# w_in's row blocks dealt to the partitions in another order, and x permuted to match

## The chip, the core and the metric

The kernel runs on one core of one Trainium2 chip. The core has a matrix engine (TensorE, PE), a vector engine (VectorE, DVE), a scalar engine (ScalarE, ACT), a general engine (GpSimd, POOL), a queue engine that issues transfers (SyncE, SP), an on-chip memory of 128 partitions (SBUF), an accumulator memory that the matrix engine writes to (PSUM), and 16 DMA engines that move data between the chip's main memory (HBM) and SBUF. The metric is the device time of one execution in microseconds (us), lower being better. The time before is the median of three runs, 216.86 us (216.77 to 216.94).

## What is computed

One decoding step for two sequences: an attention over the last 4096 positions of a key and value cache, and a small gated network whose output, passed through silu, scales the attention's. Cut to what matters:

```python
def reference(A_x, A_k_cache, A_v_cache, A_wq, A_wo, B_x, B_w_in, B_w_sp, B_b_sp, B_w_out):
    def _A_ref(x, k_cache, v_cache, wq, wo):
        W = min(4096, max(256, Sk // 4))
        q = (lambda x, *d: x.transpose(*d))((x @ wq).reshape(B, Sq, Hq, Dh), 0, 2, 1, 3)
        k = jnp.repeat(k_cache[:, :, Sk - W:, :], rep, axis=1)
        v = jnp.repeat(v_cache[:, :, Sk - W:, :], rep, axis=1)
        scores = jnp.einsum("bhqd,bhkd->bhqk", q, k) * (Dh ** -0.5)
        p = _softmax(scores, axis=-1)
        o = jnp.einsum("bhqk,bhkd->bhqd", p, v)
        return (lambda x, *d: x.transpose(*d))(o, 0, 2, 1, 3).reshape(B, Sq, Hq * Dh) @ wo
    def _B_ref(x, w_in, w_sp, b_sp, w_out):
        z = _gelu(jnp.einsum("bsd,df->bsf", x, w_in))
        z1 = z[..., :Fh]
        z2 = _layernorm(z[..., Fh:], axis=-1)
        g = jnp.einsum("ts,bsf->btf", w_sp, z2) + b_sp[None, :, None]
        return jnp.einsum("bsf,fd->bsd", z1 * g, w_out)
    xn = _layernorm(A_x, axis=-1)
    s = _A_ref(xn, A_k_cache, A_v_cache, A_wq, A_wo)
    g = _silu(_B_ref(xn, B_w_in, B_w_sp, B_b_sp, B_w_out))
    return A_x + s * g
```

The batch is 2, D is 512, there are 32 query heads over 8 key and value heads of 128, and w_in is 512 x 1792. All numbers are float32.

## The kernel before

The kernel is a stream of large loads with the computing hung on their landings. All large loads are issued by SP in one order and move through the same 16 DMA engines: w_in (`win`), w_out (`wout`), wq in three pieces, then the windows of the caches, two key heads (K) or two value heads (V) at a time, in eight units each, and at the end wo. `win`, the pieces of wq, the K and V units and wo share a ring of four buffers (`slot`), so that SP issues a load when the buffer's previous tenant has been used up. The first K buffer is free from the beginning; its issue nevertheless stands behind a wait for win's landing.

The layout of a load is a mapping from rows in HBM to partitions. For w_in (lines 120 to 122) partition p gets the rows 4p to 4p + 3 (KT is 4), one run of 4 x 1792 floats, 28,672 bytes. Both sides of that load have 128 entries in their outermost dim. The K and V loads (lines 146 to 152) interleave two heads: their source has 64 entries outermost, then 2, then a run of 8192 floats, for 128 partitions.

x is normalized on two partitions as `xn` (line 194). A matmul contracts over partitions, so x is brought to them in the same order as the weights' rows: line 197 transposes, for each k of 0 to 3, the columns 4p + k of `xn` to partition p, and line 198 copies the result from PSUM into `xnT`, a tile of 128 x 4 x 32 whose other columns are zero. `xnT` is used twice: with `win` in lines 238 to 244 (`z`, four column blocks times four k, each k to its own quarter of the PSUM partitions), and with wq in `queries` (line 268), where wq's rows have the same order.

DVE, ACT, PE and SP work strictly in the order of the program (`InOrder`, line 55); POOL's memsets are placed by a scheduler. Between line 198 and the loop over `z` DVE builds a set of small constant masks. From the units on, the order of work is written out by hand in `ORDER`. PSUM tiles made with `bank` take turns in two buffers, and `kts` tiles likewise in SBUF.

The line of nearly every instruction in the profile is L65, the helper of `InOrder`; instructions are told apart by their tiles.

Of the kernel before, what the change touches and what calls it, by code (L numbers as in the profile page):

```python
# [9 lines left out]
F32 = mybir.dt.float32  # L10
# [4 lines left out]
P = 128  # L15
# [55 lines left out]
def kernel(  # L71
# [13 lines left out]
    nc = tc.nc  # L85
    pe, dve, act, sp = (InOrder(tc, e) for e in (nc.tensor, nc.vector, nc.scalar, nc.sync))
    B, _, D = x.shape
# [5 lines left out]
    F = w_in.shape[1]  # L93
    FH = F // 2
    KT = D // P
    FC = F // G
# [10 lines left out]
    cst = ctx.enter_context(tc.tile_pool(name="cst", bufs=1))  # L107
    sb = ctx.enter_context(tc.tile_pool(name="sb", bufs=2))
    ps = ctx.enter_context(tc.tile_pool(name="ps", bufs=1, space=bass.MemoryType.PSUM))

    def slot(name, *shape):
        return ring.tile([P, *shape], F32, tag="slot", name=name)

    def bank(name, *shape):
        return ps.tile([P, *shape], F32, tag="kt", name=name, bufs=2)


    xs = sb.tile([B, D], F32, tag="ss", name="xs", bufs=1)
    act.dma_start(xs, x[:, 0, :])
    win_v = w_in.rearrange("(p k) f -> p k f", p=P)  # L120
    win = slot("win", KT, F)
    sp.dma_start(win, win_v)
    wout = kts.tile([P, FT, D], F32, tag="kts", name="wout")
    sp.dma_start(wout, w_out.rearrange("(p j) d -> p j d", p=P))
    wq_v = wq.rearrange("(p k) f -> p k f", p=P)
# [29 lines left out]
    ident = cst.tile([P, P], F32, tag="ident", name="ident")  # L155
    make_identity(nc, ident)
    selw = cst.tile([P, 60], F32, tag="selw", name="selw")
    nc.gpsimd.memset(selw, 0.0)
    xnT = cst.tile([P, KT, 32], F32, tag="xnT", name="xnT")
    nc.gpsimd.memset(xnT, 0.0)  # L160
    ones = cst.tile([P, P], F32, tag="ones", name="ones")
    nc.gpsimd.memset(ones, 1.0)
# [29 lines left out]
    rsqrt(rs, va, "x")  # L192
    xn = sb.tile([B, D], F32, tag="o", name="xn", bufs=1)
    dve.tensor_scalar(xn, xs, mv[:, 0:1], rs, op0=ALU.subtract, op1=ALU.mult)
    pt = bank("xnT_ps", KT, B)
    for k in range(KT):
        pe.transpose(pt[:, k, :], xn.rearrange("b (p k) -> b k p", k=KT)[:, k, :], ident[:B, :B])
    dve.tensor_copy(xnT[:, :, :B], pt)

    same = cst.tile([P, G, 32], F32, tag="same", name="same")  # L200
    dve.tensor_copy(same, free_ap(rowm, 0, [[0, G], [1, 32]]))
# [24 lines left out]
    for nj in (8, 16):  # L226
        nx = 32 // nj
        to = cst.tile([P, nj * P // 32 // 4, 4, nx], F32, tag=f"perm{nj}", name=f"perm{nj}")
# [9 lines left out]
    for n in range(G):  # L238
        pz = bank(f"z{n}", 512)[:, :FC]
        for k in range(KT):  # L240
            pe.matmul(
                pz[32 * k : 32 * k + 32, :], xnT[:, k, :], win[:, k, n * FC : (n + 1) * FC],
                start=True, stop=True,
            )
        if n % 2:
            dve.tensor_copy(z[:, n * FC : (n + 1) * FC], pz)
        else:
            act.activation(z[:, n * FC : (n + 1) * FC], pz, AF.Copy)
# [4 lines left out]
    pt = bank("zT_ps", 2, FT, B)  # L253
# [349 lines left out]
    for u in range(NU):  # L603
        p = Unit()
        p.u, p.m, p.kt, p.sh, p.ss, p.s, p.p, p.pT = u, None, {}, {}, {}, {}, {}, {}
        units.append(p)
    for line in ORDER.strip().split("\n"):
        for name in line.split():
            name, at = name.split(":")
# [35 lines left out]
```

## Time and profile before

| | |
|---|---|
| median of three runs | 216.86 us (216.77 to 216.94) |
| the profiled execution | 217.29 us, of which its span 215.5 us |
| PE busy | 143.2 us, 66% of the span |
| DVE busy | 126.7 us, 59% |
| ACT busy | 51.6 us, 24% |
| POOL busy | 4.5 us, 2% |
| read from HBM | 89.40 MB, 415 GB/s over the span |
| mean granted clock of PE | 0.825 |

The span runs from the first to the last instruction of the program; the execution's own time is a little longer, as it holds what lies around that. Busy shares are averages over the whole span. "Idle before, and what ended it" in square brackets behind an instruction names what the instruction last waited for. The 16 DMA engines are shown together: their share is the mean over all of them.

### The profile page before, as it was taken

The page shows a single profiled execution, that of the slowest core. Times are in us where ns is not written, and L with a number is a line of the kernel's source. Part 1 is how long each engine was busy: PE and PEld are TensorE (multiplying, and loading weights), DVE is VectorE, ACT ScalarE, POOL GpSimd, SP SyncE. Part 2 cuts the span into 40 slices and gives each one's busy share as a digit, 9 for nine tenths or more (in the row PEclk, how much of TensorE's full clock was granted, in tenths as well). Part 3 has the DMA queues.
Part 4 walks back from the last instruction along what each step waited for, and adds up shares of the span by engine and source line. Part 5 has one row for each costly group of instructions (what it writes and reads, how often), then busy time and mean ns, then how long its engine had stood idle before and what let it go on. Part 6 is the DMA issues. An engine that isn't in the chain of part 4 may idle for free.

```text
span 215.5 us, 2332 instructions
## 1 busy us (share of the span) xinstructions
PE 143.2 (66%) x900; PEld 48.1 (22%) x900; DVE 126.7 (59%) x218; ACT 51.6 (24%) x129; POOL 4.5 (2%) x17
## 2 busy tenths in 40 slices
PE   0179796833854966964991795389259917987793
PEld 0117622111120221222220231123112201232231
DVE  2611213169899799649928972993698099636011
ACT  5011103300116036033330602142051206142201
POOL 8000000000000000000000000000000000000000
PEclk9999569665998896796697599669755997996999
DMA  7999999999999999999999999999999999999990
GB/s 246 432 443 444 398 429 465 414 458 414 456 408 447 420 426 444 426 443 426 450 420 450 408 441 420 426 450 426 447 415 456 401 456 414 447 426 417 420 374 22
DMA packets 3930, 89.54 MB, mean 416 GB/s; under 512 B 446, under 2 KB 462, under 8 KB 848
## 3 DMA queue, kind: packets, MB, share of 16 engines
q1 hardware_dynamic: 3900, 89.40, 96.8%
q8 instruction: 7, 0.11, 0.2%
q14 instruction: 3, 0.02, 0.0%
q10 hardware_dynamic: 20, 0.01, 0.0%
HBM read 89.40 MB, written 0.00 MB: 415 GB/s over the span
## 4 chain that ended last, share of the span: by engine, by line
DMA 63%; PE 23%; DVE 8%; ACT 3%; issue 1%; ACTq 0%
DMA v<-in_A_v_cache_dram 42%; DMA k<-in_A_k_cache_dram 16%; PE acc L65 10%; DMA win<-in_B_w_in_dram 5%; PE sh L65 5%; DVE kts L65 4%; PE part L65 4%; PE s L65 3%; DVE pT L65 1%; ACT p L65 1%; ACT o L65 1%; DVE gate L65 1%; PE mo L65 1%; ACT ss L65 1%; DVE qb L65 1%
## 5 line engine op out<-in xcount | busy, mean ns | idle before, releaser
L65 DVE STREAM_TRANSPOSE kts<-k 128x1024 f32<-128x1024 f32 x64 | 75.6, 1218 | 29.5 <-DMA k<-in_A_k_cache_dram 29.5
L65 PE MATMUL sh<-kts,qb 128*32 128x512 f32 x256 | 41.6, 775 | 13.2 <-DVE kts L65 9.3
L65 PE MATMUL acc<-v,pT 128*32 128x512 f32 x256 | 37.4, 707 | 8.8 <-DVE pT L65 4.4
L65 ACT ACTIVATE p<-s,nb 128x512 f32<-128x512 f32 x32 | 22.5, 733 | 36.2 <-DVE nb L65 36.2
L65 ACT ACTIVATE ss<-sh 128x512 f32<-128x512 f32 x16 | 9.6, 599 | 59.1 <-PE sh L65 59.1
L65 DVE STREAM_TRANSPOSE pT<-p 128x1024 f32<-128x1024 f32 x16 | 19.6, 1225 | 2.3 <-ACT p L65 2.1
L65 PE MATMUL s<-ss,sums 128*128 128x512 f32 x32 | 18.8, 671 | 2.3 <-ACT ss L65 2.3
L65 PE MATMUL mo<-mg,joint 128*128 128x16 f32 x16 | 4.0, 327 | 23.4 <-DVE mg L65 23.4
L65 PEld LDWEIGHTS acc<-v,pT 128*32 128x32 f32 x256 | 10.5, 145 | 35.1 <-issue 27.0
L65 PEld LDWEIGHTS sh<-kts,qb 128*32 128x32 f32 x256 | 8.8, 126 | 34.2 <-issue 28.8
L65 DVE TENSOR_REDUCE m<-s 128x1 f32<-128x512 f32 x16 | 10.7, 671 | 4.2 <-PE s L65 4.2
L65 PE MATMUL q_ps<-wq,xnT 128*32 128x512 f32 x64 | 10.5, 784 | 3.5 <-DMA wq<-in_A_wq_dram 3.5
L65 ACT ACTIVATE o<-acc,wd 128x128 f32<-128x128 f32 x32 | 9.1, 368 | 15.0 <-PE acc L65 15.0
L65 PEld LDWEIGHTS mo<-mg,joint 128*128 128x128 f32 x16 | 3.2, 250 | 27.2 <-DVE mg L65 24.4
L65 PE MATMUL z<-win,xnT 128*32 128x448 f32 x32 | 5.6, 869 | 4.7 <-DMA win<-in_B_w_in_dram 4.7
L65 PE MATMUL part<-wo,oT 128*32 128x512 f32 x56 | 7.7, 596 | 1.4 <-ACT o L65 1.4
L65 PEld LDWEIGHTS s<-ss,sums 128*128 128x128 f32 x32 | 5.0, 197 | 10.3 <-issue 7.7
L65 PE MATMUL zT_ps<-rowm,z 128*128 128x2 f32 x28 | 6.6, 370 | 0.0
L65 PEld LDWEIGHTS zT_ps<-rowm,z 128*128 128x128 f32 x28 | 6.5, 325 | 0.0
L65 ACT ACTIVATION_READ_ACCUMULATOR p<-s,nb 128x1 f32 x32 | 6.5, 203 | 0.0
L65 ACT ACT_TABLE_LOAD x4 | 5.1, 1283 | 2.6 <-POOL hT L164 2.6
L65 DVE COPY z<-z 128x448 f32<-128x448 f32 x2 | 1.3, 626 | 7.5 <-PE z L65 7.5
(111 smaller groups left out, 68.4 us busy)
## 6 DMA issues: line engine op xcount, KB each, us to landing
k<-in_A_k_cache_dram SPq DMA_DIRECT2D x8, 4096.0 KB, 27.4
v<-in_A_v_cache_dram SPq DMA_DIRECT2D x8, 4096.0 KB, 29.8
wq<-in_A_wq_dram SPq DMA_DIRECT2D x1, 4096.0 KB, 24.5
wq<-in_A_wq_dram SPq DMA_DIRECT2D x2, 2048.0 KB
wo<-in_A_wo_dram SPq DMA_DIRECT2D x1, 4096.0 KB, 30.4
win<-in_B_w_in_dram SPq DMA_DIRECT2D x1, 3584.0 KB, 11.5
wo<-in_A_wo_dram SPq DMA_DIRECT2D x1, 2048.0 KB
wout<-in_B_w_out_dram SPq DMA_DIRECT2D x1, 1792.0 KB, 15.3
```

Of the source, the lines that this page charges most:

```text
L65: return self.tc.keep_in_program_order(call(*args, **kwargs))
```

## The change

The source of w_in's load gets three dims instead of two: 16 entries one block (four rows) apart, within each 8 entries 16 blocks apart, and within each the run of a block. The destination is the same tile in the same order of partitions. So partition 8e + i holds block e + 16i, where before it held block 8e + i.

The contraction over w_in needs x in the same order. A copy on DVE permutes `xn`'s columns into a new tile `xp` on two partitions, four transposes bring them to the 128 partitions, and a copy puts them into a new tile `xnS`, which is set to zero by POOL beforehand and which the matmuls with `win` read. `xnT` is still made, after it, for wq. The number of matmuls is the same but for these four transposes.

```diff
-    win_v = w_in.rearrange("(p k) f -> p k f", p=P)
+
     win = slot("win", KT, F)
-    sp.dma_start(win, win_v)
+    spaced = [[KT * F, 16], [16 * KT * F, P // 16], [1, KT * F]]
+    sp.dma_start(win.rearrange("p k f -> p (k f)"), bass.AP(tensor=w_in.tensor, offset=w_in.offset, ap=spaced))
...
     xnT = cst.tile([P, KT, 32], F32, tag="xnT", name="xnT")
+    xnS = cst.tile([P, KT, 32], F32, tag="xnS", name="xnS")
+    nc.gpsimd.memset(xnS, 0.0)
     nc.gpsimd.memset(xnT, 0.0)
...
-    pt = bank("xnT_ps", KT, B)
-    for k in range(KT):
-        pe.transpose(pt[:, k, :], xn.rearrange("b (p k) -> b k p", k=KT)[:, k, :], ident[:B, :B])
-    dve.tensor_copy(xnT[:, :, :B], pt)
+    xs = sb.tile([B, KT, 16, P // 16], F32, tag="xp", name="xp", bufs=1)
+    dve.tensor_copy(xs.rearrange("b k e i -> b e i k"), xn.rearrange("b (i e k) -> b e i k", e=16, k=KT))
+    for to, of in ((xnS, xs.rearrange("b k e i -> b k (e i)")), (xnT, xn.rearrange("b (p k) -> b k p", k=KT))):
+        pt = bank("xnT_ps", KT, B)
+        for k in range(KT):
+            pe.transpose(pt[:, k, :], of[:, k, :], ident[:B, :B])
+        dve.tensor_copy(to[:, :, :B], pt)
...
-                pz[32 * k : 32 * k + 32, :], xnT[:, k, :], win[:, k, n * FC : (n + 1) * FC],
+                pz[32 * k : 32 * k + 32, :], xnS[:, k, :], win[:, k, n * FC : (n + 1) * FC],
```

## The prediction, made before the change was run

> **What bounds the kernel now.** I read the page first: the span, the transfer rows over the slices, the queues and the chain that ended last.
>
> ```profile
> span 215.5 us, 2332 instructions
> DMA  7999999999999999999999999999999999999990
> q1 hardware_dynamic: 3900, 89.40, 96.8%
> DMA 63%; PE 23%; DVE 8%; ACT 3%; issue 1%; ACTq 0%
> ```
>
> The sixteen DMA engines are busy in every slice but the first and the last, and the chain that ended last is transfers for 63% of the span. No compute engine stands near that. So the second view is the table of stretches, which gives the bytes moved in each (last column, GB/s) and the mean busy share of the DMA engines (next to last).
>
> ```profile
> 1.00:1.50 0.50, 0.00 (x0) 0.00 (x0) 0.00 (x0) 0.00 (x0) 0.47 (x4) 1.00 0.00 0
> 1.50:2.00 0.50, 0.00 (x0) 0.00 (x0) 0.35 (x2) 0.00 (x0) 0.50 (x4) 1.00 3.29 811
> 2.00:2.50 0.50, 0.00 (x0) 0.00 (x0) 0.50 (x3) 0.00 (x0) 0.50 (x1) 1.00 0.25 57
> 2.50:3.00 0.50, 0.00 (x0) 0.00 (x0) 0.47 (x2) 0.43 (x1) 0.50 (x1) 1.00 0.17 57
> 3.00:3.25 0.25, 0.00 (x0) 0.00 (x0) 0.18 (x2) 0.25 (x1) 0.25 (x1) 1.00 0.00 0
> 3.25:3.50 0.25, 0.00 (x0) 0.00 (x0) 0.00 (x0) 0.25 (x1) 0.25 (x1) 1.00 0.54 229
> 3.50:3.75 0.25, 0.00 (x0) 0.00 (x0) 0.00 (x0) 0.25 (x1) 0.25 (x2) 1.00 1.62 688
> 3.75:4.00 0.25, 0.00 (x0) 0.00 (x0) 0.00 (x0) 0.24 (x2) 0.25 (x3) 1.00 1.61 688
> 4.00:4.25 0.25, 0.00 (x0) 0.00 (x0) 0.00 (x0) 0.23 (x2) 0.25 (x2) 1.00 0.00 0
> 4.25:4.50 0.25, 0.00 (x0) 0.00 (x0) 0.00 (x0) 0.25 (x1) 0.25 (x2) 1.00 0.80 344
> ...
> 40.00:80.00 40.00, 23.73 (x142) 6.68 (x134) 32.58 (x42) 7.58 (x20) 0.00 (x0) 0.82 1.00 432
> 80.00:120.00 40.00, 27.23 (x166) 8.11 (x169) 28.87 (x41) 10.49 (x29) 0.00 (x0) 0.78 1.00 432
> 120.00:160.00 40.00, 26.15 (x168) 8.27 (x164) 28.73 (x40) 12.93 (x35) 0.00 (x0) 0.80 1.00 432
> ```
>
> From 40 to 160 us the rate is 432 GB/s at a share of 1.00, or 27.0 GB/s an engine: nothing is to be had there but fewer bytes, and the change moves the same bytes. The first microseconds are different. w_in goes over as 128 rows of 28,672 bytes, and a short stretch credits a packet whole to the moment it begins, so GB/s times the stretch, divided by 28,672, counts the packets that begin in it. 1.50 to 2.00 gives 405 KB, 14 packets; the next two stretches give one each: sixteen, the first packet of each engine. Then 2, 6, 6 and, after a hole, 3 begin: the second packets, and in the last group a third one of the engine that was ahead. With the middle of each stretch the first packets begin at 1.84 us on average ((14 x 1.75 + 2.25 + 2.75) / 16) and the second ones at 3.78 ((2 x 3.375 + 6 x 3.625 + 6 x 3.875 + 2 x 4.375) / 16). A first packet thus took 1.94 us, where 28,672 bytes at 27.0 GB/s are 1.06. **The start costs 0.88 us an engine on average, and the engines leave it about 1.0 us apart** (second packets begin at 3.4 to 4.4). As every engine has the same bytes to move at the same rate, the one that leaves last stays last, and a load has landed only when its last engine is done.
>
> The third view is that chain in order of time, for what the end hangs on.
>
> ```profile
> 0.73 11.48 DMA win<-in_B_w_in_dram
> ...
> 150.21 32.33 DMA v<-in_A_v_cache_dram
> ...
> 206.95 3.64 PE part L65 x28
> ```
>
> win lands at 12.2, which is 4.4 plus seven packets of 1.06 and 0.4 more. The last transfer on the chain lands at 182.54; the remaining 30 us are computing. The DVE work that this computing also needs had begun with another landing:
>
> ```profile
> 172.91 1.25 DVE L65 STREAM_TRANSPOSE kts<-k 128x1024 f32<-128x1024 f32 x1 [6.66 <-DMA k<-in_A_k_cache_dram]
> ```
>
> So whatever the first load gains or loses on its slowest engine passes through the full queues to those landings and to the end, one for one.
>
> **The change part by part.** It deals w_in's blocks (four rows each) so that partition 8e + i gets block e + 16i, and permutes x alike.
>
> *What is added beside the load.* These rows show the nearest work, and what covers it.
>
> ```profile
> 1.09 0.20 POOL L160 MEMSET xnT<- 128x128 f32 x1
> 2.56 1.28 ACT L65 ACT_TABLE_LOAD   x1 [2.56 <-POOL hT L164]
> 3.07 0.14 DVE L65 TENSOR_SCALAR va<-mv 2x1 f32<-2x1 f32 x1
> 6.33 0.53 DVE L65 TENSOR_SCALAR xn<-xs,mv,rs 2x512 f32<-2x512 f32 x1
> 7.01 0.61 PE L65 MATMUL xnT_ps<-ident,xn 2*128 2x2 f32 x4 [7.01 <-DVE xn L65]
> 7.65 0.17 DVE L65 COPY xnT<-xnT_ps 128x8 f32<-128x8 f32 x1 [0.79 <-PE xnT_ps L65]
> 9.57 0.28 DVE L65 TENSOR_REDUCE at<-ident 128x2 f32<-128x128 f32 x1
> 12.35 2.47 PE L65 MATMUL z<-win,xnT 128*32 128x448 f32 x12 [4.73 <-DMA win<-in_B_w_in_dram]
> 15.62 0.62 DVE L65 COPY z<-z 128x448 f32<-128x448 f32 x1 [5.77 <-PE z L65]
> 47.34 1.19 DVE L65 TENSOR_TENSOR qb<-qa,grpm 128x1024 f32<-128x1024 f32 x1
> ```
>
> One more memset on POOL is 0.20 us. It can delay the identity and with it DVE's first work, but va is done at 3.21 and ACT's logarithm cannot begin before its table is in at 3.84, so 0.6 us of delay is free. The permuting copy of 2 x 512 on DVE is not in the trace: 0.53 by the row of xn, 1.19 by the dearest strided row, which has twice the elements; I take 0.6, nearer the first, as it has xn's shape. Four transposes more are 0.61 on PE, one copy more is 0.17 on DVE. xnS is then ready at 7.82 + 0.6 = 8.4 (9.0 at most), xnT at about 9.2, and DVE's constants end near 11.3 instead of 9.85. PE's first matmul on win waits for the load until 12.35, and DVE has nothing to do until 15.62. Cost: nothing, with 3.3 us of cover; without that cover it would be 1.4 us on z alone. Even z being late would not reach the end, for the next rows show how deep the queue is.
>
> ```profile
> SPq L65 <- DMA win<-in_B_w_in_dram: 8.8, 1, 8.8
> win<-in_B_w_in_dram SPq DMA_DIRECT2D x1, 3584.0 KB, 11.5
> wout<-in_B_w_out_dram SPq DMA_DIRECT2D x1, 1792.0 KB, 15.3
> wq<-in_A_wq_dram SPq DMA_DIRECT2D x1, 4096.0 KB, 24.5
> wq<-in_A_wq_dram SPq DMA_DIRECT2D x2, 2048.0 KB
> k<-in_A_k_cache_dram SPq DMA_DIRECT2D x8, 4096.0 KB, 27.4
> ```
>
> The only issue that hangs on win's landing is the first of k. Ahead of it stand 13,568 KB, at 432 GB/s 32 us of work, while the issue comes at 12.2: it may come 20 us later without a gap.
>
> *The issue itself.* The source becomes a pattern of three dims, as k's is.
>
> ```profile
> 0.73 0.39 SPq L65 DMA_DIRECT2D win<-in_B_w_in_dram  x1
> L65 SPq DMA_DIRECT2D k<-in_A_k_cache_dram x8: 534/535/636, 12.2 to 145.5; - x8
> ```
>
> win's issue takes 0.39 us, k's 0.535. If the longer pattern is the reason, all packets begin 0.15 us later; the bounds are 0 and 0.25 (the longest of k's). It stands ahead of the very first packet, where nothing hides it. I take +0.15.
>
> *The start.* If each engine takes eight partitions in a row, the engines began 229,376 bytes apart, and now 28,672 apart. What that does to the 0.88 us no row shows. Bounds: the slowest engine's second packet begins at 4.4, and with no stall at all it would begin at 1.84 + 1.06 = 2.9, a gain of 1.5; if the stall grew by as much again as its mean, a loss of 0.9. Between, the nearest row is the engine that got through quickest, at 3.4, which is 1.0 better than the slowest: engines under the same start can do it. I take 0.7 of that, since an even start takes away crowding and not the latency that the quickest one has too.
>
> [...]
>
> Sum: -0.7 + 0.15 = -0.55 us. The profiled execution took 217.29 us, 1.8 more than its span of 215.5 and 0.43 more than the median of 216.86; taken off that median, the forecast is **216.3 us**, and 216.7 for an execution like the profiled one.
>
> **The rivals.** *The start stays as it was:* the delay is that of a cold start, whatever the addresses. For it: even the quickest engine lost 0.5 us (3.4 less 2.9). Against it: the 1.0 us between engines, which a common latency doesn't make. Time: 216.86 to 217.0 with the issue.
>
> *Neighbours crowd more:* sixteen engines now begin within 459 KB, and if they meet in the same part of memory the stall grows, by up to its mean of 0.88. It decides once the growth exceeds the 0.3 us that a measurement can see beside the issue. For it: the trace shows that a common start is uneven. Against it: after one packet all engines run at full rate whatever they read. Time: 217.3 to 217.8.
>
> *The split collides at the destination:* this is the rival that is far on the other side. The outermost dim of the source now has 16 entries where the destination has 128, so an engine may be given eight neighbouring partitions, and if two engines then write into the same part of SBUF at a time, each runs at half rate for the whole of win. Price: 3584 KB take 8.5 us at 432 GB/s, and 17.0 at 216, so +8.5: 225.4; with collisions for a part of the eight rows, less. It decides from the first packet, and win would land near 20 instead of 12.2. [...] Against it: k's source, with 64 entries outermost, already differs from its 128 partitions and runs at 432.
>
> [...]
>
> **How the numbers follow.** An uneven start cured: 0.37. Start as it was: 0.17. Neighbours crowd more: 0.16. Collision at the destination: 0.30. The forecast is the first, with its own range of 215.6 to 216.4 (a gain of 1.25 down to 0.45). About 0.2%, 0.43 us, is what a measurement of this kernel can tell from no change. Faster than that has 0.37, within it 0.19 (the second case and the small end of the third), slower 0.44. As cases of both signs hold most of the chance, the range for 8 times in 10 must reach into the fourth: 215.8 to 225.5.
>
> **What would show it.** In the table of stretches after: second packets that begin by 3.7 at the latest and closer together, win landing at about 11.5, every later landing earlier by as much, PE still waiting for win and not for xnS. A landing of win at 12.2 to 12.4 is the second case; 12.6 to 13.3 with full rate from the second packet the third; about 216 GB/s until 20 us the fourth. The forecast is wrong too if win lands early and the chain that ended last no longer passes through a load of v near 182, so that the gain is lost in the computing behind it.

## The result, and the profile after

The changed kernel takes 225.54 us (median of 4 runs, 225.32 to 225.55) where the kernel before takes 216.81 us (4 runs, 216.60 to 216.94): slower by 4.0%, ratio 1.0399 with a 95% interval of 1.0387 to 1.0412. That is 8.73 us more. The profiled execution took 225.53 us.

The page of the changed kernel, its span, transfer rows and queues:

```profile
span 223.7 us, 2344 instructions
...
DMA  7979989999899999999999999999999899999991
GB/s 165 246 164 287 492 381 422 460 428 464 381 463 445 404 460 404 439 463 385 457 428 422 463 393 448 457 398 457 416 431 458 387 463 439 410 460 404 428 395 42
...
q1 hardware_dynamic: 3900, 89.40, 96.9%
```

The GB/s row of the kernel before:

```profile
GB/s 246 432 443 444 398 429 465 414 458 414 456 408 447 420 426 444 426 443 426 450 420 450 408 441 420 426 450 426 447 415 456 401 456 414 447 426 417 420 374 22
```

The packets and bytes are the same, and the share in which the DMA engines are busy is the same as well (96.9% and 96.8%). Only the GB/s row tells the two kernels apart: its first four slices, some 22 us, move 165, 246, 164 and 287 GB/s where they moved 246, 432, 443 and 444. Here a busy share of 96.9% does not tell how fast the packets get through.

The stretches of the changed kernel, with busy share and GB/s in the last two columns:

```profile
2.00:2.50 0.50, 0.00 (x0) 0.00 (x0) 0.50 (x3) 0.00 (x0) 0.50 (x2) 1.00 3.27 860
2.50:3.00 0.50, 0.00 (x0) 0.00 (x0) 0.47 (x2) 0.29 (x1) 0.50 (x1) 1.00 0.22 57
...
3.75:4.00 0.25, 0.00 (x0) 0.00 (x0) 0.00 (x0) 0.24 (x2) 0.25 (x3) 1.00 3.90 803
4.00:4.25 0.25, 0.00 (x0) 0.00 (x0) 0.00 (x0) 0.23 (x2) 0.25 (x3) 1.00 3.34 688
4.25:4.50 0.25, 0.00 (x0) 0.00 (x0) 0.00 (x0) 0.25 (x1) 0.25 (x1) 1.00 1.68 344
...
5.00:19.00 14.00, 1.02 (x8) 0.96 (x8) 4.11 (x24) 0.70 (x2) 0.16 (x1) 1.00 0.95 197
...
80.00:120.00 40.00, 32.02 (x208) 9.71 (x212) 32.83 (x45) 11.45 (x31) 0.00 (x0) 0.87 1.00 432
```

The first of the long stretches, in the kernel before:

```profile
5.00:19.00 14.00, 7.26 (x42) 3.12 (x42) 4.59 (x25) 1.65 (x4) 0.01 (x1) 1.00 0.98 423
```

From 5 to 19 us, while only win is moving, the rate is 197 GB/s at a busy share of 0.95, so some 207 GB/s at full share, and a packet of 28,672 bytes takes 2.2 us on one of sixteen engines; from 80 us on it is 432 as before. In the same way as in the prediction, the packets that begin can be counted: sixteen by 3.00 us, sixteen more between 3.75 and 4.50, and then a hole before the next (0 GB/s from 4.50 to 5.00). What followed the load, in the order of time:

```profile
0.73 0.70 SPq L65 DMA_DIRECT2D win<-in_B_w_in_dram  x1
...
8.45 0.17 DVE L65 COPY xnS<-xnT_ps 128x8 f32<-128x8 f32 x1 [0.74 <-PE xnT_ps L65]
...
20.74 0.58 SPq L65 DMA_DIRECT2D k<-in_A_k_cache_dram  x1
...
20.86 1.72 PE L65 MATMUL z<-win,xnS 128*32 128x448 f32 x8 [11.98 <-DMA win<-in_B_w_in_dram]
```

xnS is there at 8.62 us; PE waits for win until 20.86, where it had waited until 12.35. The pieces of the chain that ended last carry the delay to the end:

```profile
0.73 19.99 DMA win<-in_B_w_in_dram
...
180.39 29.81 DMA wo<-in_A_wo_dram
```

win lands at 20.72 instead of 12.21, which is 8.5 us later; the spans of the two profiled executions differ by 8.2. After win the rate is about that of before (437, 432, 435 and 431 GB/s in the four stretches of 40 us from 40 to 200) and nothing is caught up, as the queues are full to the end, now on the chain with wo's first load, which lands at 210.2.

### The profile page after: what moved, and what is told of

It is laid out like the page before. It is cut to its first block, busy times and chain, and to the rows that moved or that the text cites. A ratio compares the mean times of both kernels' runs of the same rounds, so it can differ in the third digit from the quotient of the medians.

```text
span 223.7 us, 2344 instructions
## 1 busy us (share of the span) xinstructions
PE 146.5 (65%) x904; PEld 48.7 (22%) x904; DVE 127.5 (57%) x220; ACT 51.7 (23%) x129; POOL 4.6 (2%) x18
## 3 DMA queue, kind: packets, MB, share of 16 engines
q1 hardware_dynamic: 3900, 89.40, 96.9%
## 4 chain that ended last, share of the span: by engine, by line
DMA 60%; PE 18%; DVE 16%; ACT 3%; issue 1%; ACTq 0%
DMA k<-in_A_k_cache_dram 38%; DMA wo<-in_A_wo_dram 13%; DVE kts L65 10%; DMA win<-in_B_w_in_dram 9%; PE sh L65 6%; PE acc L65 4%; PE part L65 3%; PE s L65 3%; ACT p L65 2%; DVE pT L65 2%; DVE m L65 1%; ACT ss L65 1%; DVE gate L65 1%; DVE nb L65 1%; DVE qb L65 0%
## 5 line engine op out<-in xcount | busy, mean ns | idle before, releaser
L65 PE MATMUL sh<-kts,qb 128*32 128x512 f32 x256 | 44.5, 824 | 13.3 <-DVE kts L65 9.5
L65 PE MATMUL acc<-v,pT 128*32 128x512 f32 x256 | 35.9, 683 | 6.6 <-DVE pT L65 3.8
L65 PE MATMUL s<-ss,sums 128*128 128x512 f32 x32 | 19.8, 702 | 2.3 <-ACT ss L65 2.3
L65 PEld LDWEIGHTS acc<-v,pT 128*32 128x32 f32 x256 | 9.9, 144 | 32.9 <-issue 23.3
L65 PE MATMUL z<-win,xnS 128*32 128x448 f32 x32 | 5.7, 885 | 12.0 <-DMA win<-in_B_w_in_dram 12.0
```

Source lines behind the costliest of these rows:

```text
L65: return self.tc.keep_in_program_order(call(*args, **kwargs))
```

## The experiments

**Where the rows land, or where they come from.** Two theories make the same time. By the first, an engine now gets eight neighbouring partitions, and two engines at a time hinder each other where the rows land, in SBUF. By the second, engines that read neighbouring rows hinder each other in HBM. The first experiment keeps the pattern of 16 x 8 rows and puts the starts of the 16 entries 229,376 bytes apart, as the prediction had those of the engines in the kernel before. (A pattern of exactly the old rows would be two dims again; hence the overlap.)

```diff
-    sp.dma_start(win, win_v)
+    near = [[8 * KT * F, 16], [KT * F - 64, 8], [1, KT * F]]
+    sp.dma_start(win.rearrange("p k f -> p (k f)"), bass.AP(tensor=w_in.tensor, offset=w_in.offset, ap=near))
```

> The kernel before with win's source as 16 x 8 rows, where the engines begin 229,376 bytes apart as in the kernel before; the 8 rows of an engine begin 28,416 bytes apart instead of 28,672, so that each overlaps the next by 256 bytes and w_in is read slightly shifted. If the loss comes from where the rows land (an engine gets eight neighbouring partitions and two engines share a way into SBUF): packets of about 2.2 us, win lands at 20 to 21 us, 225.5 us in all, as after the change. If it comes from neighbouring rows being read at a time: packets of 1.06 us, landing at 12.2 to 12.6, 216.9 us.

Measured: 225.88 us (one run), win landing at 21.2, and in its stretches:

```profile
5.00:19.00 14.00, 0.61 (x4) 0.55 (x4) 3.28 (x22) 0.70 (x2) 0.01 (x1) 1.00 0.95 199
```

The rate is that of the changed kernel (199 GB/s and 197, both at 0.95) although the entries start far apart. The second experiment is the other half of the test: neighbouring rows, but 32 x 4 of them.

```diff
-    spaced = [[KT * F, 16], [16 * KT * F, P // 16], [1, KT * F]]
+    spaced = [[KT * F, 32], [32 * KT * F, P // 32], [1, KT * F]]
...
-    xs = sb.tile([B, KT, 16, P // 16], F32, tag="xp", name="xp", bufs=1)
-    dve.tensor_copy(xs.rearrange("b k e i -> b e i k"), xn.rearrange("b (i e k) -> b e i k", e=16, k=KT))
+    xs = sb.tile([B, KT, 32, P // 32], F32, tag="xp", name="xp", bufs=1)
+    dve.tensor_copy(xs.rearrange("b k e i -> b e i k"), xn.rearrange("b (i e k) -> b e i k", e=32, k=KT))
```

> The changed kernel with 32 x 4 rows instead of 16 x 8: partition 4c + j gets block c + 32j, x permuted to suit. Rows read at a time are again neighbours, but the outermost 32 entries can be dealt in groups of four partitions. If the loss comes from where the rows land: packets of 1.06 us after the first, win lands at 11.5 to 12.7, 216.3 to 217.2 us; where in that range tells whether neighbouring starts shorten the slow first packets at all. If it comes from neighbouring rows being read at a time, or from any source of three dims that is not k's: landing near 20, about 225 us.

Measured: 217.29 us (11 runs) beside 216.99 of the kernel before (21 runs), ratio 1.0012, interval 1.0003 to 1.0021. Its stretches:

```profile
2.00:2.50 0.50, 0.00 (x0) 0.00 (x0) 0.50 (x3) 0.00 (x0) 0.50 (x2) 1.00 1.50 516
2.50:3.00 0.50, 0.00 (x0) 0.00 (x0) 0.47 (x2) 0.33 (x1) 0.50 (x1) 1.00 1.10 401
...
3.25:3.50 0.25, 0.00 (x0) 0.00 (x0) 0.00 (x0) 0.25 (x1) 0.25 (x1) 1.00 1.24 459
3.50:3.75 0.25, 0.00 (x0) 0.00 (x0) 0.00 (x0) 0.25 (x1) 0.25 (x1) 1.00 1.09 459
3.75:4.00 0.25, 0.00 (x0) 0.00 (x0) 0.00 (x0) 0.24 (x2) 0.25 (x3) 1.00 0.81 344
4.00:4.25 0.25, 0.00 (x0) 0.00 (x0) 0.00 (x0) 0.23 (x2) 0.25 (x3) 1.00 1.36 573
...
5.00:19.00 14.00, 7.81 (x44) 3.09 (x44) 5.31 (x27) 1.76 (x4) 0.17 (x1) 1.00 0.99 422
```

The rate is full: 422 GB/s at a share of 0.99, beside 423 at 0.98 in the kernel before. Neighbouring rows are not the cause; the second theory falls, and so does one that blames any pattern of three dims.

**The partitions alone.** The third experiment has nothing unusual in its source: two transfers of two dims, each over half of the partitions.

```diff
-    sp.dma_start(win, win_v)
+    sp.dma_start(win[: P // 2], win_v[: P // 2])
+    sp.dma_start(win[P // 2 :], win_v[P // 2 :])
```

> The kernel before with win loaded in two transfers, partitions 0 to 63 and then 64 to 127, each of two dims and the rows as before. If two engines that write into one part of SBUF halve each other, and 64 neighbouring partitions reach only half of the ways in: about 206 to 216 GB/s until win is in, landing at 19.5 to 21, 225 us. If the loss hangs on the source or on the form with 16 entries: 432 GB/s, landing at 12.2 to 12.7, 216.9 to 217.2 us.

Measured: 226.10 us (one run), win in by 21.3. So the same loss can be had with ordinary sources, by loading half of the partitions at a time. A later experiment cut once more, into four transfers of 32 partitions.

```diff
-    sp.dma_start(win, win_v)
+    for p in range(0, P, 32):
+        sp.dma_start(win[p : p + 32], win_v[p : p + 32])
```

> The kernel before with win loaded in four transfers of 32 partitions each (two rows for an engine), rows as before. [...] If engines hinder each other the more the closer together their partitions are: packets of 4 us or more, win in by 35 to 40, 240 us or more.

Measured: 226.04 us (one run), win in by 21.0. The stretches of the two, halves first:

```profile
5.00:10.00 5.00, 0.61 (x4) 0.55 (x4) 3.28 (x22) 0.62 (x2) 0.01 (x1) 1.00 0.90 184
5.00:19.00 14.00, 0.61 (x4) 0.55 (x4) 3.28 (x22) 0.62 (x2) 0.01 (x1) 1.00 0.95 197
```

```profile
5.00:7.50 2.50, 0.47 (x4) 0.50 (x4) 1.12 (x5) 0.58 (x2) 0.01 (x1) 1.00 0.90 184
...
10.00:12.50 2.50, 0.00 (x0) 0.00 (x0) 0.00 (x0) 0.00 (x0) 0.00 (x0) 1.00 0.86 185
12.50:15.00 2.50, 0.00 (x0) 0.00 (x0) 0.00 (x0) 0.00 (x0) 0.00 (x0) 1.00 1.18 241
```

Divided by the busy share, these rows give 204 to 215 GB/s: the engines have the same half rate on 64 partitions and on 32, so they do not hinder each other the more the closer together their partitions are. What sets a limit that is the same for 32 neighbours and for 64, and half of the rate of 128, no view shows. That win comes in several transfers is not the reason: the last kernel below loads it in two as well, each over all 128 partitions, and moves at full rate, 414 GB/s at 0.97.

```profile
5.00:10.00 5.00, 2.67 (x10) 1.16 (x10) 3.10 (x22) 0.55 (x2) 0.16 (x1) 1.00 0.97 414
```

That the source of 16 x 8 rows suffers from the same thing is concluded from the same rate (207 GB/s): no run had 16 entries and rows that go to partitions farther apart.

**Dose.** If it is the half rate that costs, the loss must be in proportion to the bytes, wherever the load stands.

```diff
-    sp.dma_start(wout, w_out.rearrange("(p j) d -> p j d", p=P))
+    dealt = [[FT * D, 16], [16 * FT * D, P // 16], [1, FT * D]]
+    sp.dma_start(wout.rearrange("p j d -> p (j d)"), bass.AP(tensor=w_out.tensor, offset=w_out.offset, ap=dealt))
```

> The kernel before with w_out's load, not w_in's, dealt as 16 x 8 rows: partition 8e + i gets the row block e + 16i of seven rows, while the hidden values that multiply them keep the old order, so that the product is left without its right partners. win is loaded as before and lands at 12.2. If eight neighbouring partitions for an engine halve the rate of the load that is so split, wherever it stands: wout's 1792 KB take 8.9 us at 206 GB/s instead of 4.25, and the whole gets longer by 4.6 us, 221.6 us. If the loss needs the cold start of the first load or is fixed for a kernel: 217 us, or 225 again.

Measured: 221.52 us (one run), with the kernel before at 216.94: 4.58 more, for half of win's bytes. win landed at 12.8 us, not at the 12.2 expected, and the rate is already 310 GB/s from 10 to 12.5 us. It is low around wout's load, 215 GB/s from 12 to 19 us, and 432 again on average over slices 9 to 38 of its GB/s row (44 to 209 us):

```profile
5.00:10.00 5.00, 0.61 (x4) 0.55 (x4) 3.28 (x22) 0.57 (x2) 0.01 (x1) 1.00 0.96 414
...
12.00:19.00 7.00, 6.05 (x38) 2.40 (x39) 1.32 (x3) 1.09 (x2) 0.00 (x0) 1.00 1.01 215
...
GB/s 251 418 245 280 459 391 432 432 455 406 465 412 447 426 429 447 418 438 413 459 400 459 412 459 415 441 441 418 444 418 443 418 453 406 453 409 459 392 393 41
```

**What x costs.** The changed kernel with the old load; everything that was added for x still runs.

```diff
-    spaced = [[KT * F, 16], [16 * KT * F, P // 16], [1, KT * F]]
-    sp.dma_start(win.rearrange("p k f -> p (k f)"), bass.AP(tensor=w_in.tensor, offset=w_in.offset, ap=spaced))
+    sp.dma_start(win, w_in.rearrange("(p k) f -> p k f", p=P))
...
-                pz[32 * k : 32 * k + 32, :], xnS[:, k, :], win[:, k, n * FC : (n + 1) * FC],
+                pz[32 * k : 32 * k + 32, :], xnT[:, k, :], win[:, k, n * FC : (n + 1) * FC],
```

> The changed kernel with win loaded as before and z reading xnT: what is left of the change is the permuting copy, the four transposes, the copy into xnS (which nothing reads) and the memset. All theories: hidden behind the wait for win, 216.6 to 217.1 us. If something of it is on the path after all: 217.5 or more.

Measured: 216.91 us beside 216.99, ratio 0.9993, interval 0.9985 to 1.0002. The permuting costs nothing that can be measured.

**The start.** The 32 x 4 kernel allowed a look at the gain that the forecast was built on. Its first packets begin at 2.47 us on average (9 by 2.50, 7 after), its second ones at 3.77: a first packet takes 1.30 us, and took 1.94 before. Against that stands that it begins 0.63 later by the same count of stretches. Is the packet shorter because of the rows, or because it is later? The next kernel has the same form, with the starts far apart.

```diff
-    sp.dma_start(win, win_v)
+    near = [[4 * KT * F, 32], [KT * F - 64, 4], [1, KT * F]]
+    sp.dma_start(win.rearrange("p k f -> p (k f)"), bass.AP(tensor=w_in.tensor, offset=w_in.offset, ap=near))
```

> The kernel before with win's source as 32 x 4 rows in three dims, the engines' starts as far apart as in the kernel before; the four rows of a group begin 28,416 bytes apart, so that each overlaps the next by 256 bytes and w_in is read slightly shifted. Issue 0.65 us and first packets at 2.45, as with 32 spaced rows. If neighbouring starts are what shortened the first packets from 1.84 to 1.30 us there: 1.84 here, second packets at about 4.3 on average, 217.4 to 217.6 us. If the later start alone shortened them: 1.30, second packets at 3.75, 217.2 to 217.3.

Measured: 217.35 us beside 216.94, ratio 1.0020, interval 1.0011 to 1.0029. Its issue and its stretches:

```profile
0.73 0.65 SPq L65 DMA_DIRECT2D win<-in_B_w_in_dram  x1
```

```profile
2.00:2.50 0.50, 0.00 (x0) 0.00 (x0) 0.50 (x3) 0.00 (x0) 0.50 (x1) 1.00 3.35 803
2.50:3.00 0.50, 0.00 (x0) 0.00 (x0) 0.47 (x2) 0.34 (x1) 0.50 (x1) 1.00 0.32 115
...
3.75:4.00 0.25, 0.00 (x0) 0.00 (x0) 0.00 (x0) 0.24 (x2) 0.25 (x3) 1.00 1.62 688
4.00:4.25 0.25, 0.00 (x0) 0.00 (x0) 0.00 (x0) 0.23 (x2) 0.25 (x2) 1.00 1.08 459
4.25:4.50 0.25, 0.00 (x0) 0.00 (x0) 0.00 (x0) 0.25 (x1) 0.25 (x2) 1.00 1.07 459
4.50:4.75 0.25, 0.00 (x0) 0.00 (x0) 0.00 (x0) 0.25 (x1) 0.25 (x3) 1.00 0.53 229
```

14 and 2 first packets begin at 2.31 on average, 6, 4, 4 and 2 second ones at 4.16: 1.84 us for a first packet, 0.54 more than with neighbouring rows, at nearly the same start. (For the kernel before, where the expectation says 1.84, the count gives 1.94; in the two other kernels with the old load, the one with w_out's rows dealt anew and the one with the work for x alone, it gives 1.83 and 1.86.) In these two profiles, one of each kernel, it is the rows that differ. In the times the two kernels, 1.0012 and 1.0020, are not told apart, as their intervals overlap. The last kernel tried to have both, the early issue of two dims and neighbouring first rows:

```diff
-    sp.dma_start(win, win_v)
+    sp.dma_start(win[:, 0], w_in[:P])
+    sp.dma_start(win[:, 1:], w_in[P:].rearrange("(p k) f -> p k f", p=P))
...
+    rest = xn[:, P:].rearrange("b (p k) -> b k p", k=KT - 1)
+    pt = bank("xnS_ps", KT, B)
+    for k in range(KT):
+        pe.transpose(pt[:, k, :], rest[:, k - 1, :] if k else xn[:, :P], ident[:B, :B])
+    dve.tensor_copy(xnS[:, :, :B], pt)
...
-                pz[32 * k : 32 * k + 32, :], xnT[:, k, :], win[:, k, n * FC : (n + 1) * FC],
+                pz[32 * k : 32 * k + 32, :], xnS[:, k, :], win[:, k, n * FC : (n + 1) * FC],
```

> win in two transfers of two dims over all 128 partitions: row p to partition p first (917 KB, engines begin 28,672 bytes apart if each begins four partitions after the last), then rows 128 + 3p to 130 + 3p; x transposed to suit by slices, without a permuting copy. If neighbouring starts shorten the first packets and the early issue of two dims (0.39 us, packets from 1.75 on) is kept: both gains together, 0.3 to 0.6 us under the kernel before, 216.4 to 216.7. If the start is the same whatever the rows, 216.9 to 217.2, the more by the smaller first packets.

Measured: 217.11 us beside 216.94, ratio 1.0008, interval 0.9999 to 1.0017. A miss: the gain did not come. Its stretches show where it failed to come:

```profile
1.50:2.00 0.50, 0.00 (x0) 0.00 (x0) 0.35 (x2) 0.00 (x0) 0.50 (x4) 1.00 0.92 166
2.00:2.50 0.50, 0.00 (x0) 0.00 (x0) 0.50 (x3) 0.00 (x0) 0.50 (x2) 1.00 0.46 100
2.50:3.00 0.50, 0.00 (x0) 0.00 (x0) 0.47 (x2) 0.44 (x1) 0.50 (x1) 1.00 0.84 330
```

Its packets are 7,168 bytes, so 166 GB/s in the first row are 83 KB, under 12 packets, and 100 are 7. In the second row sixteen engines at 27.0 GB/s would have begun 30 packets: the start is early, as before, and held up, as before. With an early start, then, neighbouring rows did not help, though its first packets are a quarter as long, too, so that more than the rows differs; what lets the later start of the 32 x 4 kernel profit from them stays open. No version beat the kernel before.

## Why the prediction was wrong

*Which case.* The time is that of the fourth rival, the collision at the destination, which was given 0.30 against 0.37 for the forecast, and 225.4 us against the 225.54 measured. The forecast's sum, -0.7 + 0.15, holds a start and an issue and nothing for the rate behind them, which it kept at 27.0 GB/s an engine; that rate halved, packets took 2.2 us instead of 1.06, and this is the 8.5 us. It was kept out of the sum by one argument, and that is the step that failed: "Against it: k's source, with 64 entries outermost, already differs from its 128 partitions and runs at 432". That row was taken as evidence that a source whose outermost dim differs from the destination's does no harm. It shows this for 64 entries, and the runs for 32 (422 GB/s from 5 to 19 us); with 16 the rate halves (197). In the place of that step the runs put a limit between 16 and 32 entries. Why it lies there is not shown, as no view here shows which engine moves which rows; shown are the rates at 16, 32 and 64 entries and at 128, 64 and 32 partitions.

A second weakness stands in the prediction's part on the start. "If each engine takes eight partitions in a row" was written for the old load and the new alike, and was not held against the old rate: had engines on eight neighbours each collided, the old load could not have run at 432. How far apart the engines began in the kernel before, 229,376 bytes or less, no view shows.

*The price.* 8.5 us, from 3584 KB at half of 432 GB/s; measured 8.73 in the medians and 8.51 in win's landing. The halved rate is right, the close agreement partly luck: at the measured 207 GB/s 3584 KB take 17.7 us, 9.2 more than at 432. But the first of an engine's eight packets was slow before, too (1.94 us, and 1.78 after, by the same count), so that seven were slowed, by 1.15 us each, 8.1 in all, and the first packets began at 2.28 instead of 1.84. The route to the end, one for one through full queues, held: beside the kernel with the work for x alone, which has the old load, win lands 8.7 us later and wo's first load 8.6 (12.0 and 201.6 there, 20.7 and 210.2 after the change), and the same route gave wout's 4.6 us, measured 4.58.

*The issue.* +0.15 us, bounds 0 and 0.25, by the length of k's issue. Wrong in size: the issue took 0.70 us instead of 0.39, and with 32 x 4 rows, at full rate and with the old starts, the whole was 0.20% slower, 0.41 us by the medians. k's 0.535 us was the wrong row: 16 x 8 rows took 0.70 us as the first issue and, for wout, 0.66 as the second. And the first packets came later by more than the issue was lengthened (0.44 us for 0.31 in the changed kernel, 0.47 for 0.27 with 32 x 4 rows and far starts), which no row of before could show. The third rival's upper end leaves the issue out: with it and the 0.88 the time would be 217.9, not 217.8.

*The start.* -0.7 us for the slowest engine. In the changed kernel the half rate hides it. With 32 x 4 rows, the last second packet begins by 4.25 us where it did so by 4.50 before, and a first packet is 0.54 us shorter on average than in the same form with far starts. So the effect is partly there, but not at its forecast size, and the later start takes it back: second packets begin at 3.77 us on average, where they began at 3.78. The 32 x 4 kernel, the nearest one at full rate, is not faster than the kernel before (ratio 1.0012). Its win lands at 12.1 us, between the 12.0 and the 12.2 of the two kernels with the old loads, and yet the whole is 0.30 us longer; where that arises stays open.

*The work for x.* Nothing, with xnS ready at 8.4: it was ready at 8.62, and the kernel that has this work alone is not slower.

*The range.* It ended at 225.5, 0.04 us short of the time. The bound lay 0.1 us above the rival's time of 225.4, to which the issue had not been added.

## What to carry to other kernels

Before the layout of a load is changed, look at the outermost dim of its source: here, for 128 partitions, 32, 64 and 128 entries kept 422 to 432 GB/s and 16 halved it (207 at full share), and so did a destination of 64 partitions or of 32 (204 to 215). A busy share of 0.95 did not show this; the bytes per stretch did, 197 GB/s where there had been 423. In this kernel, bound by transfers through full queues, a slower load at the beginning (win, wout) was paid at the end nearly whole (8.73 and 4.58 us).

## What the runs showed that was not expected

The form of the load changes the time of the very first issue: two dims over 128 partitions took 0.39 us, 32 x 4 rows 0.65 and 16 x 8 rows 0.70, and with these two the first packets began about half a microsecond later. The third dim is not the whole of it: the two issues over 64 partitions, of two dims, took 0.58 and 0.59, the four over 32 partitions 0.40 to 0.85, and wout's issue right behind win, whose form did not change, took 0.57 instead of 0.41 behind the long forms. Under half rate the busy share from 5 to 19 us is 0.95, hardly less than the 0.98 of the kernel before. And four transfers of 32 partitions cost no more than two of 64, 226.04 and 226.10 us.
